# Three plain pairs instead of four in the second sequence chunk, P and Q stored in two halves, weights' jobs later

## The chip, the cores and the metric

The kernel runs on one core of one Trainium2 chip. The metric is the device time of one execution in microseconds (us), median of several runs. A profiled execution gives the trace; its span runs from the first to the last instruction. TensorE is written PE here, VectorE DVE, ScalarE ACT, GpSimd POOL and SyncE SP, as in the profile.

## The reference, cut to what matters

```python
xn = layernorm(x)                                    # x: 2048 x 512
a = einsum("bsd,ed->bse", xn, dft_hid_re)
b = einsum("bsd,ed->bse", xn, dft_hid_im)
s = einsum("ts,bse->bte", dft_seq_re, a) - einsum("ts,bse->bte", dft_seq_im, b)
h = relu(einsum("bsd,df->bsf", xn, w1) + b1) ** 2    # F = 1792
g = silu(einsum("bsf,fd->bsd", h, w2) + b2)
out = x + s * g
```

All is float32. `s` takes the sequence transform as a 2048 x 2048 product and the hidden transform as a 512 x 512 product, each with a real and an imaginary matrix.

## The kernel before

**Number format.** Every operand is split in a high part (a copy on ACT, `split_hi`, L136) and a low part (source minus high, on DVE, `split_lo`, L139), both in a format that PE multiplies fast. A product of two operands is three passes: high x high, high x low, low x high.

**Seven products.** Nearly all matrix products go as a 2 x 2 block product by seven multiplications (`PRODUCTS`) instead of eight. That needs sums of the blocks of both operands beforehand, made on DVE, and sums of the seven results afterwards, in the "closing" steps (`closing_of`).

**Stages.** (1) Layer norm of `x`, with chunk 0 of the sequence transform multiplied plainly meanwhile. (2) Chunks 1 to 7 of the sequence transform: `c` counts chunks of 256 output rows of both sequence matrices, `j` eight pairs of 128-row tiles of `x`. The sequence matrices are multiplied with `x` first; the results P and Q go to DRAM (`PQD`). (3) The Y units multiply P and Q with the hidden matrices (`WDP`). (4) The H units: first dense layer. (5) The second dense layer, SiLU, the product and the residual. The change lies in stage 2; its last effects reach the first Y units.

**Chunk 0 and the x sums.** After chunk 0 the sums of the `x` blocks must be made, for the pairs 0 to 3 in one go (`side[0]`, four steps of a generator) and for 4 to 7 in another (`side[1]`), and each pair's sums must be split (`split_sums(j)`, 1024 elements a partition, ACT and DVE), before a pair can take part in seven products.

**Chunk 1 ("second sequence chunk").** To give DVE time for that, the pairs in `MIXED` (4, 5, 6, 7) are multiplied plainly in chunk 1: `plain_step(j)`, eight block products, 48 matmuls of 256 columns, which need no sums, only a split of 1024 elements. The other pairs (0, 1, 2, 3) go by seven products, 42 matmuls, and each needs three sums of the matrix blocks (`step_sums`, L300, L302, L303) and a split of 1792 elements (`step_split`). The loop over `MIXED` (L605 to L634) lists by hand which preparations are issued at each plain pair.

**Chunks 2 to 7.** The loop over `steps` (L638 to L675): a step issues the matmuls of its pair, then the sums for two steps on (`step_sums(n + 2)`), the split for the next step (`step_split(n + 1)`), the load for four steps on (`step_load(n + 4)`, into a tile `u` of three buffers), then a closing step of the chunk before, then jobs of the table `EARLY`. The split operands use two buffers, `ga` and `gb`, in turn by the parity of `j`, so the split of a step can begin only when PE has finished the step before the present one. All engines take their instructions in this order; one that waits holds what is queued behind it on its engine. DMA loads and stores of this stage are all issued on SP.

**Closing and store.** At the last pair of a chunk (`LAST`) the result tile `e` is taken anew. ACT copies one bank to it and, but for the last chunk, three banks to `left` buffers; DVE does two closing steps, and the rest follow in the next chunk, one a step by `LATER` and `LATER_1` (the latter for the closing of chunk 1, which has one step more). At `j == 5` of that next chunk, one DMA of 1 MB stores `e` (L660). `e` is one buffer, so the next chunk's closing waits for that store to land. The layout of `e` has C12 and C11 in its first half, C22 and C21 in its second.

**Jobs of `EARLY`.** `d0` to `d3`: the hidden matrices, `v0`, `v1`, `v6`: parts of `w1`. Each (`weight`, L435) has five steps: load, first sum, other two sums, split and store of three blocks (768 elements a partition), split and store of four blocks of sums (1024). The split operands lie in `wd0` or `wd1`. `p0` to `p3` load transformed hidden matrices back (`load_wd`, L495; `p0` into `wd0`, `p1` into `wd1`) in two halves. `y0` to `y2` (`y_early`, L480) prepare the first P and Q tiles for the Y units: load, sums, split of three blocks, split of four.

**Into the Y units.** After the step (7,7) come two closing steps and the last three steps of `y2`; then the Y units (`YUnit`), whose first group of 12 matmuls is followed on ACT by a "seed" copy and on DVE by sums.

Of the kernel before, what the change touches and what calls it, by code (L numbers as in the profile page):

```python
# [16 lines left out]
NJ, NP = NS // 2, NF // 2  # L17
CW = 256
NC = S // CW
TC = 512  # L20
NTC = S // TC
WARM = 8, 5
MIXED = 4, 5, 6, 7

REST = NP - 4

# [8 lines left out]


EARLY = {
# [8 lines left out]
}  # L46
LATER = {0: 1, 1: 1, 2: 1, 3: 1, 4: 1}
LATER_1 = {0: 1, 1: 1, 2: 1, 3: 1, 4: 1, 5: 1}


Y_SIDE = (
# [73 lines left out]
C21, C11, C22, C12 = range(4)  # L125
# [5 lines left out]
def fnet_gated_kernel(ctx, tc, x, xt, ct, wd, w1, w2, b1, b2, out):  # L131
    nc = tc.nc
    ctx.enter_context(tc.manual_schedule(engines=None))

    def split_hi(hi, lo, src):
        nc.scalar.activation(hi, src, AF.Copy)  # L136
# [4 lines left out]
    def split(*parts):  # L141
        split_hi(*parts)
        split_lo(*parts)
# [15 lines left out]
    PQD = [dram.tile([P, 2, 4, 256], F32, name=f"pqd{c}") for c in range(NC)]  # L159
# [30 lines left out]
    XC = [None] * NJ  # L190
# [85 lines left out]
    def split_sums(j):  # L276
        s = xn32[j].rearrange("p h (b n) -> p (h b) n", b=2)
        split(XC[j][:, S2:S1 + 1, HI, :], XC[j][:, S2:S1 + 1, LO, :], s)
# [9 lines left out]
    def plain_parts(c, j, hs=slice(0, 2)):  # L288
        if (c, j) not in part:
            part[c, j] = operand_buf("g" + "ab"[j % 2], f"g{c}_{j}", 0 if c or j == NJ - 1 else 3 if j in TURNED else 1, (2, 4, CW))  # L290
        g, r = part[c, j], raw[c, j]
        s = slice(2 * hs.start, 2 * hs.stop)
        return g[:, HI, s], g[:, LO, s], r[:, s]
# [11 lines left out]
    def sums_a(*operands):  # L305
        list(sums_a_steps(*operands))

    def sums_a_steps(t, a21, a11_a22, a11, a12, turned=False):

        nc.vector.tensor_tensor(t[:, 0:2], a21.to_broadcast([P, 2, 256]), a11_a22, op=ALU.subtract)  # L310
        yield
        if turned:
            nc.vector.tensor_tensor(t[:, 2], a11, t[:, 1], op=ALU.subtract)
            nc.vector.tensor_tensor(t[:, 3], a12, t[:, 2], op=ALU.subtract)  # L314
        else:
            nc.vector.tensor_tensor(t[:, 2], t[:, 1], a11, op=ALU.subtract)
            nc.vector.tensor_tensor(t[:, 3], t[:, 2], a12, op=ALU.add)  # L317

    def sums_rows(t, r, turned=False):

        sums_a(t, r[:, C12:C12 + 1], r[:, C11:C22 + 1], r[:, C11], r[:, C21], turned)

    def sums_w1_steps(t, r):
        return sums_a_steps(t, r[:, 0:1], r[:, 1:4:2], r[:, 1], r[:, 2], True)
# [10 lines left out]
    def step_sums(n):  # L335
        if n < len(steps):
            u = raw[steps[n]]
            sums_b(u[:, 4:8], u)
# [44 lines left out]
    def mm(ps, w, mv, first, last):  # L383

        ps = ps.rearrange("p (i d t) -> p d i t", i=2, d=2)
        for d in range(2):
            for a_, b_ in PASSES:
                nc.tensor.matmul(ps[:, d], w[:, a_, d * P:(d + 1) * P], halves(mv(b_)),  # L388
                                 start=first and d == 0 and (a_, b_) == (HI, HI),
                                 stop=last and (a_, b_) == (LO, HI), skip_group_check=True)  # L390
# [17 lines left out]
    ms = {}  # L408
# [9 lines left out]
                mm(ms[k], XC[j][:, a], lambda b_: g[:, b_, q], j == MIXED[0] and not i, k == Z and j == MIXED[-1] and i == 1)  # L418

    one, two = slice(0, 1), slice(1, 2)  # L420
    steps = [(1, j) for j in range(NJ) if j not in MIXED] + [(c, j) for c in range(2, NC) for j in range(NJ)]
    order = [(0, j) for j in range(NJ)] + [(1, j) for j in MIXED] + steps
    making, makers = {}, {}

    def go(*names):


        for v in names:
            if v[0] == "h" and int(v[1:]) >= NTC * NP:
                continue  # L430
            if v not in making:
                making[v] = makers[v[0]](int(v[1:]))
            next(making[v])
# [46 lines left out]
    def y_early(n):  # L480

        k = n // 2
        r = buf(f"pq{k}0", [P, 4, 256], f"yr{n}")
        load_pq(n, r)
        yield
        t = buf(f"pq{k}1", [P, 4, 256], f"yt{n}")
        sums_rows(t, r, True)
        yield
        g = yop[n] = operand_buf(Y_HOME[n // 2 % 3][n % 2], f"yg{n}", 1 if n % 6 else 3)
        split(g[:, HI, 4:7], g[:, LO, 4:7], r[:, 0:3])  # L490
        yield
        split(g[:, HI, 0:4], g[:, LO, 0:4], t)
        yield
# [51 lines left out]
    g = plain_parts(0, 1)  # L545
# [3 lines left out]
    side = sums(0), sums(1)  # L549
    load_c(0, 3)  # L550
    load_x(4)
    for j in range(1, NJ):
# [31 lines left out]
        g = plain_parts(*order[j + 1])  # L584
# [16 lines left out]
    def some(steps_, n):  # L601
        for _ in range(n):
            next(steps_)

    for i, j in enumerate(MIXED):  # L605
        if i == 0:
            some(side[0], 2)
            split(*plain_parts(1, MIXED[1]))
            split_sums(0)
            for k in range(ND):  # L610
                plain_out(k)
            for k in range(2):
                nc.sync.dma_start(PQD[0][:, k].rearrange("p k n -> p (k n)"), plain[k])
            some(side[1], 1)
        elif i == 1:
            split_sums(1)
            split(*plain_parts(1, MIXED[2]))
            some(side[1], 1)
            split_sums(2)
            go("d0")  # L620
        elif i == 2:
            split_sums(3)
            some(side[1], 1)
            split(*plain_parts(1, MIXED[3]))
            step_sums(0)
            go("d0", "d0")
        else:
            step_sums(1)
            some(side[1], 1)
            step_split(0)  # L630
            split_sums(4)
            split_sums(5)
        plain_step(j)
        load_c(*order[NJ + i + 4])  # L634

    LAST = {(c, max(j for c_, j in steps if c_ == c)) for c in range(1, NC)}
    closing = None
    for n, s in enumerate(steps):  # L638
        c, j = s
        if c > 1 and j == 0:  # L640
            ms = {}
        for k, tag in banks(c).items():
            if k not in ms:
                ms[k] = bank(tag, f"m{k}_{c}")
        g = part.pop(s)
        for p in FIRST if j == 0 and c > 1 else ORDER:
            a, b = PRODUCTS[p]
            mm(ms[p], XC[j][:, a], lambda b_: g[:, b_, b], j == 0 and (c > 1 or p in (1, 5, 6, 7)), s in LAST)
        step_sums(n + 2)
        step_split(n + 1)  # L650
        if n < 2:
            split_sums(6 + n)
        if n == 0:
            e = buf("e", [P, 2048], "c1")
            copy(chunk_part(e)(C22), halves(ms[Z]))
        step_load(n + 4)
        if closing:
            some(closing, (LATER_1 if c == 2 else LATER).get(j, 0))
            if j == max(LATER_1):
                nc.sync.dma_start(PQD[c - 1].rearrange("p h k n -> p (h k n)"), e)  # L660
                closing = None
        if s in LAST:
            if c > 1:
                e = buf("e", [P, 2048], f"c{c}")
            room = {}
            if c < NC - 1:
                room = buf("pq10", [P, 2, 512], f"left{c}")
                room = {7: room[:, 0], 5: room[:, 1], 3: buf("pq11", [P, 512], f"left3_{c}")}
            closing = closing_of(chunk_part(e), ms, room, c == 1)
            some(closing, 2)  # L670
        if s == (2, 4):
            nc.vector.transpose(stats_t, stats.rearrange("p m h j -> p (m h j)"))
            for q in range(4):
                nc.sync.dma_start(rows[:, q * 32:(q + 1) * 32], stats_t[q * 32:(q + 1) * 32, :])
        go(*EARLY.get(s, ()))  # L675
# [326 lines left out]
    for u in range(2, NC):  # L1002
        n = 2 * u + 2
# [41 lines left out]
    for n in range(NTC * NP):  # L1045
        unit = HUnit(n)
        first, second, later = H_SIDE.get(n, ((), (), ()))
# [15 lines left out]
        if n == NTC * NP - 1:  # L1063
            ms = Banks(0)
# [22 lines left out]
    for n in range(NTC * NP):  # L1087
        c, p = divmod(n, NP)
        last = c == NTC - 1
        if n and not last and p == 0:  # L1090

            ms = Banks(c)
            for k in (2, 4, 5):
                bias(ms[k], k)
        elif last and p == 0:

            ms = {k: bank(t, f"m{k}_last") for k, t in
                  {1: "b20", 2: "b21", 6: "b30", 7: "b31", 5: "bb", 3: "ba"}.items()}
# [27 lines left out]
        if p == NP - 1 and not last:  # L1126
            e = buf("e", [P, 4, 512], f"z{c}")
# [16 lines left out]
    e = buf("u", [P, 4, 512], f"z{c}")  # L1144
# [95 lines left out]
```

## Time and profile before

| | us |
|---|---|
| median of 3 runs | 676.29 (676.10 to 677.19) |
| profiled execution, its time | 673.96 |
| profiled execution, its span | 672.1 |
| PE busy | 663.7 |
| DVE busy | 608.0 |
| ACT busy | 381.0 |

A line of the timeline gives the start of a run of like instructions, its length, engine, source line, operation, the tiles as out<-in, the shapes and the count; in square brackets, the idle time of the engine ahead of it and what ended that idle time. Lengths of instructions that follow each other without a gap overlap a little, since an engine starts the next before the last has drained; so a price is best read from start to start. A line of a helper such as L139 or L388 stands for all uses of the helper; the tile names tell them apart. In the table of DMA issues the last number is the median time from issue to landing.

### The profile page before, as it was taken

To read this page: it belongs to the slowest core of one execution; us is meant where nothing else is said; L and a number is where in the kernel's file an instruction comes from. 1 tells how busy PE (TensorE), PEld (TensorE's weight loads), DVE (VectorE), ACT (ScalarE), POOL (GpSimd) and SP (SyncE) were. 2 spreads that over 40 slices of the span, in tenths; PEclk is the share of its full clock that TensorE was granted. 3 is DMA by queue.
4 is the path that set the end of the run, shared out by engine and by line. 5 is a ranking of instruction groups with operands and counts; after the bars stand their busy time and mean duration, and the time that the engine had idled before them with its cause. 6 is when DMAs were issued, how large, how long until landed. Compare 5 with 4: busy or idle time off the path is not lost.

```text
span 672.1 us, 13519 instructions
## 1 busy us (share of the span) xinstructions
PE 663.7 (99%) x5605; PEld 651.5 (97%) x5605; DVE 608.0 (90%) x844; ACT 381.0 (57%) x516; POOL 8.8 (1%) x11
## 2 busy tenths in 40 slices
PE   8999999999999999999999999999999999999997
PEld 5889999999999999999899999999999999999997
DVE  7998999899989999998799988977887889999997
ACT  6855563535445454544365547788778765454451
POOL 0000000000000000000000000000000000101010
PEclk9999999999999999999999999999999999999999
DMA  8735264948659485879488668576755866677775
GB/s 284 234 105 186 87 219 145 325 138 285 238 184 352 150 282 193 280 271 319 157 298 279 201 188 299 199 262 214 267 182 196 328 241 211 179 232 194 215 204 157
DMA packets 51741, 150.85 MB, mean 224 GB/s; under 512 B 4960, under 2 KB 19552, under 8 KB 50272
## 3 DMA queue, kind: packets, MB, share of 16 engines
q1 hardware_dynamic: 43568, 129.28, 57.6%
q10 hardware_dynamic: 6208, 18.88, 7.1%
q0 software_dynamic: 1904, 1.84, 1.9%
q8 instruction: 44, 0.72, 0.4%
q14 instruction: 17, 0.14, 0.1%
HBM read 101.98 MB, written 47.99 MB: 223 GB/s over the span
## 4 chain that ended last, share of the span: by engine, by line
PE 89%; DVE 6%; DMA 2%; ACT 2%; issue 1%; SPq 0%; DVEq 0%; ACTq 0%
PE m L388 34%; PE m_o L905 15%; PE r_B L799 13%; PE r_A L799 9%; PE pq_b L399 4%; PE r_C L799 4%; PE r_D L799 4%; PE m_last L905 4%; PE pq_bb L399 1%; DMA pqd<-c 1%; DVE g L139 1%; DMA x<-in_x 1%; DVE c L373 1%; DVE xc L139 1%; DVE xn L273 1%
## 5 line engine op out<-in xcount | busy, mean ns | idle before, releaser
L388 PEld LDWEIGHTS m<-g,xc 128*128 128x128 f32 x2376 | 270.1, 188 | 0.9 <-DVE g L139 0.5
L388 PE MATMUL m<-g,xc 128*128 128x256 f32 x2376 | 270.6, 276 | 0.3 <-DVE g L139 0.3
L136 ACT ACTIVATE g<-u 128x1792 fp32r<-128x1792 f32 (+2 forms) x65 | 101.6, 1564 | 132.4 <-PE m L388 85.3
L139 DVE TENSOR_TENSOR g<-u,g 128x1792 fp32r<-128x1792 f32 (+2 forms) x66 | 120.0, 1819 | 9.1 <-ACT g L136 8.9
L905 PE MATMUL m_o<-w,g 128*128 128x256 f32 x882 | 100.5, 276 | 0.0
L905 PEld LDWEIGHTS m_o<-w,g 128*128 128x128 f32 x882 | 100.3, 188 | 0.0
L136 ACT ACTIVATE g<-hr 128x1792 fp32r<-128x1792 f32 (+2 forms) x31 | 48.2, 1565 | 40.0 <-DVE hr L317 17.8
L799 PE MATMUL r_B<-xT,w 128*128 128x256 f32 x504 | 66.5, 276 | 0.0
L799 PEld LDWEIGHTS r_B<-xT,w 128*128 128x128 f32 x504 | 61.5, 188 | 0.0
L139 DVE TENSOR_TENSOR g<-hr,g 128x1792 fp32r<-128x1792 f32 (+2 forms) x31 | 56.7, 1838 | 2.9 <-ACT g L136 2.8
L799 PE MATMUL r_A<-xT,w 128*128 128x256 f32 x336 | 43.1, 276 | 0.0
L399 PE MATMUL pq_b<-g,xc 128*128 128x512 f32 x144 | 41.2, 392 | 1.4 <-DVE small L247 1.4
L799 PEld LDWEIGHTS r_A<-xT,w 128*128 128x128 f32 x336 | 40.3, 188 | 0.2 <-DVE xT L139 0.2
L799 PE MATMUL r_B<-wdp,yg 128*128 128x256 f32 x288 | 36.0, 277 | 1.4 <-ACT r_B L146 1.2
L300 DVE TENSOR_TENSOR u<-u 128x512 f32<-128x512 f32 x52 | 35.6, 685 | 0.8 <-DMA u<-in_ct 0.7
L799 PEld LDWEIGHTS r_B<-wdp,yg 128*128 128x128 f32 x288 | 34.1, 188 | 1.8 <-ACT r_B L146 1.4
L399 PEld LDWEIGHTS pq_b<-g,xc 128*128 128x128 f32 x144 | 26.7, 188 | 8.1 <-ACT g L136 2.2
L905 PE MATMUL m_last<-w,g 128*128 128x256 f32 x294 | 33.5, 276 | 0.0
L905 PEld LDWEIGHTS m_last<-w,g 128*128 128x128 f32 x294 | 33.4, 188 | 0.0
L139 DVE TENSOR_TENSOR yg<-yraw,yg 128x1792 fp32r<-128x1792 f32 x13 | 26.2, 2018 | 0.8 <-ACT yg L136 0.8
L136 ACT ACTIVATE yg<-yraw 128x1792 fp32r<-128x1792 f32 x13 | 22.2, 1710 | 7.9 <-DVE yraw L314 7.3
L302 DVE TENSOR_TENSOR u<-u 128x256 f32<-128x256 f32 x52 | 22.1, 425 | 1.8
(185 smaller groups left out, 835.0 us busy)
## 6 DMA issues: line engine op xcount, KB each, us to landing
u<-in_ct SPq DMA_DIRECT2D x63, 512.0 KB, 3.8
hd<-h ACTq DMA_DIRECT2D x28, 512.0 KB, 5.1
hr<-hd SPq DMA_DIRECT2D x28, 512.0 KB, 3.7
pqd<-c SPq DMA_DIRECT2D x7, 1024.0 KB, 7.6
wdp<-wdd SPq DMA_DIRECT2D x8, 896.0 KB, 7.2
yraw<-pqd SPq DMA_DIRECT2D x13, 512.0 KB, 5.7
w<-w1d SPq DMA_DIRECT2D x6, 896.0 KB, 8.1
y<-y ACTq DMA_DIRECT2D x8, 512.0 KB, 4.9
```

The source lines that it names most:

```text
L136: nc.scalar.activation(hi, src, AF.Copy)
L139: nc.vector.tensor_tensor(lo, src, hi.bitcast(F32), op=ALU.subtract)
L273: nc.vector.tensor_tensor(s[:, :, to], s[:, :, a], s[:, :, b], op=op)
L300: nc.vector.tensor_tensor(t[:, 0:2], r[:, 0:1].to_broadcast([P, 2, 256]), r[:, 1:3], op=ALU.add)
L302: nc.vector.tensor_tensor(t[:, 2], t[:, 1], r[:, 1], op=ALU.add)
L373: nc.vector.tensor_tensor(part_(to), halves(room.get(m, ms[m])), part_(frm), op=op)
L388: nc.tensor.matmul(ps[:, d], w[:, a_, d * P:(d + 1) * P], halves(mv(b_)), start=first and d == 0 and (a_, b_) == (HI, HI), stop=last and ( ...
L399: nc.tensor.matmul(accs[k], w, part[0, j][:, b_, 2 * h:2 * h + 2], start=j == 0 and h == 0 and (a_, b_) == (HI, HI), stop=j == NJ - 1 and ...
L799: nc.tensor.matmul(self.region(REGION[k]), w, mv, start=i == 0 and k in (1, 7), stop=i == len(ops) - 1, skip_group_check=True)
L905: nc.tensor.matmul(m[:, i * 256:(i + 1) * 256], ready[n][:, a_, H_SLOT[a], i * P:(i + 1) * P], W2[p][:, b_, b], start=p == 0 and i == 0 an ...
```

## The change

- In chunk 1 the pairs 4, 5 and 6 stay plain, and five pairs go by seven products, in the order 1, 0, 3, 2, 7 (`SEVEN`), which keeps the parities in turn.
- The splits of the `x` sums move: those of pairs 0 and 1 are issued at the first plain pair, 2 at the second, 3 at the third, and the rest during steps 1 to 5 of the loop over `steps`, by `SUMS_AT`: 7, 4, 5, and 6 (in the first step of chunk 2).
- The weights' jobs begin later: only the load of `d0` is issued in chunk 1, and the rest of `d0` starts at (2,2). The whole table `EARLY` follows, up to (7,0).
- The sums of `y_early` become two steps.
- The closing of chunk 1 takes two steps at `j == 1`, so that every closing is through at `j == 4`, and its first half at `j == 3`. `e` is stored in two halves of 512 KB, at `j == 3` and `j == 4`.

```diff
-MIXED = 4, 5, 6, 7
+MIXED = 4, 5, 6
+SEVEN = 1, 0, 3, 2, 7
+SUMS_AT = {1: 7, 2: 4, 3: 5, 5: 6}
...
 EARLY = {
-    (1, 2): ("d0", "d1"), (2, 0): ("d0",), (2, 1): ("d1",), (2, 3): ("d1",), (2, 4): ("d1", "d2"), (2, 6): ("d1",),
-    (3, 0): ("d2",), (3, 1): ("d2",), (3, 2): ("d2", "d3"), (3, 4): ("d2",), (3, 5): ("d3",), (3, 6): ("d3", "d3", "v0"),
-    (4, 1): ("d3",), (4, 2): ("v0",), (4, 3): ("p1",), (4, 4): ("v0",), (4, 6): ("v0", "v1"), (4, 7): ("p1",),
-    (5, 0): ("v0",), (5, 1): ("v1",), (5, 3): ("v1",), (5, 4): ("v1", "v6"), (5, 6): ("v1",),
-    (6, 0): ("v6",), (6, 1): ("v6",), (6, 2): ("v6", "y1"), (6, 4): ("v6",), (6, 6): ("y1", "p0"),
-    (7, 0): ("p0",),
-    (7, 1): ("y1", "p3"), (7, 2): ("p3",), (7, 3): ("y1", "y0", "p2"), (7, 4): ("y2", "p2"), (7, 5): ("y0", "y0"),
-    (7, 6): ("y0",), (7, 7): ("y2", "y2", "y2"),
+    (2, 2): ("d0",), (2, 3): ("d0",), (2, 5): ("d0", "d1"), (2, 6): ("d0",), (3, 0): ("d1",), (3, 1): ("d1",),
+    (3, 2): ("d1", "d2"), (3, 4): ("d1",), (3, 5): ("d2",), (3, 6): ("d2", "d2", "d3"), (4, 1): ("d2",), (4, 2): ("d3",),
+    (4, 4): ("d3",), (4, 5): ("d3", "v0"), (4, 6): ("d3",), (4, 7): ("p1",), (5, 0): ("v0",), (5, 1): ("v0", "p1"),
+    (5, 2): ("v0", "v1"), (5, 4): ("v0",), (5, 5): ("v1",), (5, 6): ("v1", "v1", "v6"), (6, 1): ("v1",), (6, 2): ("v6",),
+    (6, 4): ("v6",), (6, 5): ("v6", "y1"), (6, 6): ("v6",), (6, 7): ("p0",), (7, 0): ("y1", "p0"),
+    (7, 1): ("y1", "p3"), (7, 2): ("y1", "p3"), (7, 3): ("y0", "p2",), (7, 4): ("y1", "y2", "p2"), (7, 5): ("y0", "y0"),
+    (7, 6): ("y0", "y0"), (7, 7): ("y2", "y2", "y2", "y2"),
 }
 LATER = {0: 1, 1: 1, 2: 1, 3: 1, 4: 1}
-LATER_1 = {0: 1, 1: 1, 2: 1, 3: 1, 4: 1, 5: 1}
+LATER_1 = {0: 1, 1: 2, 2: 1, 3: 1, 4: 1}
...
-steps = [(1, j) for j in range(NJ) if j not in MIXED] + [(c, j) for c in range(2, NC) for j in range(NJ)]
+steps = [(1, j) for j in SEVEN] + [(c, j) for c in range(2, NC) for j in range(NJ)]
...
         t = buf(f"pq{k}1", [P, 4, 256], f"yt{n}")
-        sums_rows(t, r, True)
+        first = sums_rows_steps(t, r, True)
+        next(first)
+        yield
+        list(first)
         yield
...
     for i, j in enumerate(MIXED):
         if i == 0:
             some(side[0], 2)
+            some(side[1], 1)
             split(*plain_parts(1, MIXED[1]))
             split_sums(0)
+            split_sums(1)
             for k in range(ND):
                 plain_out(k)
             for k in range(2):
                 nc.sync.dma_start(PQD[0][:, k].rearrange("p k n -> p (k n)"), plain[k])
+        elif i == 1:
+            step_sums(0)
+            split(*plain_parts(1, MIXED[2]))
+            split_sums(2)
             some(side[1], 1)
-        elif i == 1:
-            split_sums(1)
-            split(*plain_parts(1, MIXED[2]))
-            some(side[1], 1)
-            split_sums(2)
-            go("d0")
-        elif i == 2:
-            split_sums(3)
-            some(side[1], 1)
-            split(*plain_parts(1, MIXED[3]))
-            step_sums(0)
-            go("d0", "d0")
         else:
             step_sums(1)
             some(side[1], 1)
             step_split(0)
-            split_sums(4)
-            split_sums(5)
+            split_sums(3)
+            go("d0")
...
         step_sums(n + 2)
         step_split(n + 1)
-        if n < 2:
-            split_sums(6 + n)
+        if n == 0:
+            some(side[1], 1)
+        elif n in SUMS_AT:
+            split_sums(SUMS_AT[n])
...
         if closing:
             some(closing, (LATER_1 if c == 2 else LATER).get(j, 0))
-            if j == max(LATER_1):
-                nc.sync.dma_start(PQD[c - 1].rearrange("p h k n -> p (h k n)"), e)
+            if j in (3, 4):
+                q = slice((j - 3) * 1024, (j - 2) * 1024)
+                nc.sync.dma_start(PQD[c - 1][:, j - 3].rearrange("p k n -> p (k n)"), e[:, q])
+            if j == 4:
                 closing = None
```

More of the change, by code (lines that the diff above doesn't have):

```diff
@@ L317, in sums_a_steps, with sums_rows_steps, sums_rows @@
             nc.vector.tensor_tensor(t[:, 3], t[:, 2], a12, op=ALU.add)
-    def sums_rows(t, r, turned=False):
-        sums_a(t, r[:, C12:C12 + 1], r[:, C11:C22 + 1], r[:, C11], r[:, C21], turned)
+    def sums_rows_steps(t, r, turned=False):
+        return sums_a_steps(t, r[:, C12:C12 + 1], r[:, C11:C22 + 1], r[:, C11], r[:, C21], turned)
+    def sums_rows(*operands):
+        list(sums_rows_steps(*operands))
     def sums_w1_steps(t, r):
@@ L630, in fnet_gated_kernel @@
             step_split(0)
-            split_sums(4)
-            split_sums(5)
+            split_sums(3)
+            go("d0")
         plain_step(j)
         load_c(*order[NJ + i + 4])
-    LAST = {(c, max(j for c_, j in steps if c_ == c)) for c in range(1, NC)}
+    LAST = {(1, SEVEN[-1])} | {(c, NJ - 1) for c in range(2, NC)}
     closing = None
@@ L647, in fnet_gated_kernel @@
             a, b = PRODUCTS[p]
-            mm(ms[p], XC[j][:, a], lambda b_: g[:, b_, b], j == 0 and (c > 1 or p in (1, 5, 6, 7)), s in LAST)
+            mm(ms[p], XC[j][:, a], lambda b_: g[:, b_, b], (c > 1 and j == 0) or (not n and p in (1, 5, 6, 7)), s in LAST)
         step_sums(n + 2)
         step_split(n + 1)
-        if n < 2:
-            split_sums(6 + n)
+        if n == 0:
+            some(side[1], 1)
+        elif n in SUMS_AT:
+            split_sums(SUMS_AT[n])
         if n == 0:
```

## The prediction, made before the changed kernel ran

> **What bounds the kernel.** I read the engines' busy time first, then the chain that ended last. A step is written (chunk, x pair).
>
> ```profile
> PE 663.7 (99%) x5605; PEld 651.5 (97%) x5605; DVE 608.0 (90%) x844; ACT 381.0 (57%) x516; POOL 8.8 (1%) x11
> PE 89%; DVE 6%; DMA 2%; ACT 2%; issue 1%; SPq 0%; DVEq 0%; ACTq 0%
> ```
>
> TensorE (PE) is the bound, and the vector engine (DVE) runs close behind. So time can come only from fewer matmuls or from places where PE waited. The pace of PE without waits is in the chain's pieces (start, length):
>
> ```profile
> 536.82 97.94 PE m_o L905 x864
> ```
>
> 97.94 / 864 = 0.11336 us for a matmul of 256 columns: 5.44 for a plain pair (48), 4.76 for a pair by seven products (42), 1.36 for a group of 12. I held every stretch against that. The stretches that are too long:
>
> First, PE in the second chunk (timeline: start, length), and the scalar engine's (ACT) high-part pass, which is released when PE has finished a step and so marks the steps' ends:
>
> ```profile
> 51.62 26.81 PE L388 MATMUL m<-g,xc 128*128 128x256 f32 x235
> 78.74 5.44 PE L388 MATMUL m<-g,xc 128*128 128x256 f32 x44 [0.31 <-DVE g L139]
> ```
> ```profile
> 73.64 1.71 ACT L136 ACTIVATE g<-u 128x1792 fp32r<-128x1792 f32 x1 [0.57 <-ACT xc L136]
> 78.40 1.70 ACT L136 ACTIVATE g<-u 128x1792 fp32r<-128x1792 f32 x1 [1.62 <-PE m L388]
> 83.92 1.71 ACT L136 ACTIVATE g<-u 128x1792 fp32r<-128x1792 f32 x1 [2.87 <-PE m L388]
> ```
>
> From 73.64 to 78.40 is 4.76, as it should be; from 78.40 to 83.92 is 5.52, **0.76 lost**. PE waited for DVE's low-part pass of (1,1):
>
> ```profile
> 75.15 0.68 DVE L300 TENSOR_TENSOR u<-u 128x512 f32<-128x512 f32 x1
> ...
> 76.67 2.02 DVE L139 TENSOR_TENSOR g<-u,g 128x1792 fp32r<-128x1792 f32 x1
> 78.60 1.22 DVE L139 TENSOR_TENSOR xc<-xn,xc 128x1024 fp32r<-128x1024 f32 x1
> 79.73 0.69 DVE L300 TENSOR_TENSOR u<-u 128x512 f32<-128x512 f32 x1
> ```
>
> DVE is back to back here, and start to start gives its prices: the sums of a step 1.52, a low pass of 1792 elements 1.93, one of 1024 elements 1.13.
>
> Second, where chunk 2 ends (ACT):
>
> ```profile
> 126.76 1.71 ACT L136 ACTIVATE g<-u 128x1792 fp32r<-128x1792 f32 x1 [2.11 <-issue]
> 130.74 0.60 ACT L146 ACTIVATE c<-m 128x512 f32<-128x512 f32 x1 [2.28 <-DMA pqd<-c]
> ...
> 136.57 1.70 ACT L136 ACTIVATE g<-u 128x1792 fp32r<-128x1792 f32 x1 [1.66 <-PE m L388]
> 141.69 1.71 ACT L136 ACTIVATE g<-u 128x1792 fp32r<-128x1792 f32 x1 [3.42 <-PE m L388]
> ```
>
> Three steps took 14.93 for 14.28, **0.65 lost**: ACT's first copy of the closing sums waited until the store of the chunk before had left the buffer `e`; the bank behind that copy is the one (3,0) multiplies into first.
>
> Third, the same store at the end of chunk 7, at the start of the Y units (PE, then SP, ACT, DVE):
>
> ```profile
> 322.41 1.67 PE L799 MATMUL r_A<-wdp,yg 128*128 128x256 f32 x12
> 323.91 1.52 PE L799 MATMUL r_D<-wdp,yg 128*128 128x256 f32 x12
> 326.61 1.63 PE L799 MATMUL r_B<-wdp,yg 128*128 128x256 f32 x12 [1.18 <-ACT r_B L146]
> ...
> 332.57 1.65 PE L799 MATMUL r_B<-wdp,yg 128*128 128x256 f32 x12 [0.25 <-DVE y L809]
> 334.06 1.52 PE L799 MATMUL r_A<-wdp,yg 128*128 128x256 f32 x12
> ```
> ```profile
> 312.47 0.44 SPq L660 DMA_DIRECT2D pqd<-c  x1
> ```
> ```profile
> 321.75 0.60 ACT L146 ACTIVATE c<-m 128x512 f32<-128x512 f32 x1 [6.03 <-DMA pqd<-c]
> ...
> 325.23 1.06 ACT L136 ACTIVATE yg<-yt 128x1024 fp32r<-128x1024 f32 x1 [2.14 <-DVE yt L314]
> 326.19 0.37 ACT L146 ACTIVATE r_B<-r_A 128x256 f32<-128x256 f32 x1
> ```
> ```profile
> 322.39 1.29 DVE L373 TENSOR_TENSOR c<-m,c 128x512 f32<-128x512 f32 x2 [4.41 <-ACT c L146]
> ...
> 328.98 3.20 DVE L373 TENSOR_TENSOR c<-m,c 128x512 f32<-128x512 f32 x5
> 332.10 0.41 DVE L809 TENSOR_TENSOR y<-r_B,y 128x256 f32<-128x256 f32 x1
> ```
>
> Seven groups of 12 from 322.41 to 334.06 took 11.65 for 9.52, **2.13 lost**. Store at 312.47, ACT held 6.03 until 321.75, DVE idle 4.41 behind it, the preparation of y2 late by that much, the seed copy r_B behind it late, and the sum at 332.10 behind five closing sums late.
>
> **The change, part by part.**
>
> *Matmuls.* One plain pair of 48 becomes one pair of 42: 6 x 0.11336 = **0.68 less** on PE.
>
> *Work beside it.* The pair costs DVE one more group of sums and a low pass of 1792 for one of 1024: 1.52 + 0.80 = 2.32, and ACT some 0.7 by the same ratio. It is free only if DVE stays ahead of PE, which now comes to the seven-product steps one plain step earlier. I ran DVE's new order through by these prices, from its first pass of the chunk:
>
> ```profile
> 52.91 1.23 DVE L139 TENSOR_TENSOR g<-u,g 128x1024 fp32r<-128x1024 f32 x1 [1.98 <-ACT g L136]
> ```
>
> One x sum now fits into the 1.98 idle ahead of it. Then to the low pass of (1,1): two plain passes, three of the x sums' low passes, two x sums (seven of 1.13), two groups of step sums (3.04) and the pass (1.93), 12.9, which with two waits of some 0.3 on ACT ends near 66.4. PE wants it at 51.62 + 3 x 5.44 = 67.94. After that a step of DVE is 1.52 + 1.93 + one pass or x sum of 1.13 = 4.58 in 4.76, and the low pass cannot end before ACT's high pass: 0.25 after the step's start, plus 1.71, plus 1.93, so 3.9 into a step, 0.86 before PE wants it. The 0.76 goes, because two of the six low passes of x sums (1.13 each) that stood ahead of the second such step now stand behind it, and the weight sums (1.5) have left the chunk. Late next would be the same pass, by whatever exceeds 0.86.
>
> The load of (1,0) stands behind the stores of P and Q of chunk 0, which come one ACT pass (1.0) later than before, so it goes at about 57.2 for 56.22 (SP); then the landing times of such loads and stores:
>
> ```profile
> 56.22 0.41 SPq L286 DMA_DIRECT2D u<-in_ct  x1
> ```
> ```profile
> u<-in_ct SPq DMA_DIRECT2D x63, 512.0 KB, 3.8
> pqd<-c SPq DMA_DIRECT2D x7, 1024.0 KB, 7.6
> ```
>
> It lands near 61.0; DVE wants it at 61.8. No cost, and 1.5 more of margin at (1,1).
>
> *Chunks 2 to 7.* Weight jobs keep their instructions and transfers, two to eight steps later each; the Y job's sums are cut in two with the same three instructions. In chunk 2 the x sums' pass of pair 6 takes the place of a weight pass of equal size. Chunk 5 gets the job pattern that chunk 3 had and keeps; its densest step (two weight parts, 1.8, on 3.45) has light ones on both sides. Chunk 3 before, by ACT's high passes four steps apart:
>
> ```profile
> 146.47 1.71 ACT L136 ACTIVATE g<-u 128x1792 fp32r<-128x1792 f32 x1 [2.34 <-PE m L388]
> 165.46 1.71 ACT L136 ACTIVATE g<-u 128x1792 fp32r<-128x1792 f32 x1 [2.27 <-PE m L388]
> ```
>
> 18.99 for 19.04: nothing lost, so nothing is to be expected of chunk 5. Cost 0; the cover is PE's step, and if it went, the excess over 0.86 in a step would show.
>
> *The stores.* Six more issues on SP, of about 0.4 each, while SP waits for DVE anyway; behind each half in SP's queue are the step's weight jobs and the next load, which waits four us longer for a low pass. The first half is issued two steps earlier, the last one step (4.76) earlier, so the last of chunk 6 at about 307.7. Landing times of all transfers to and from this tensor (min/median/max):
>
> ```profile
> DMA to landing us min/median/max: 2.6/6.2/9.2
> ```
>
> Even at 9.2 it has left `e` by 316.9; ACT wants `e` at about 318.7, when the first product of (7,7) is done. So ACT's 6.03 goes, and DVE is some 3.5 earlier: in us from the units' start it has its two first closing sums done at -1.8, y2's sums at -0.3, y2's passes (one waits 1.0 for ACT) at 1.9, y3's sums at 3.4, the five closing sums at 6.6. The seed copy follows its product at once; the sum that PE waited for follows product 5 (6.8) at 7.4, where PE wants its bank at 8.16. **2.13 goes**, and with the same wait at chunk 2's end the **0.65**. Next late would be the low pass of y3 (1.93 more), at 9.3 where unit 1 starts at 9.5.
>
> *The sum.* 0.68 + 0.76 + 0.65 + 2.13 = 4.22. The profiled execution spans 672.1 and took 673.96, so it would take 669.7; the median of the runs is 676.29, 2.3 above it, and I take the difference over: **672.1**.
>
> The Trainium skill (Trainium Kernel Development and Optimization, Performance Expectations) calls matmul busy time a bad metric, because matmuls are pipelined. Read by the idle marks of the matmul rows alone, the stalls are 0.31 + 1.18 + 0.25 = 1.74 and the sum 2.42; by the starts it is 4.22, and this trace agrees with the rule: the wait marked 0.31 cost a step 0.76.
>
> **Rivals.**
>
> *Half of it.* Only what the matmul rows mark as idle returns: 0.68 + 1.74 = 2.42, 673.9. For it: restart costs may appear elsewhere, and y3 has 0.2 of margin. Against: spacing of starts is time.
>
> *The store is not what holds ACT.* The wait is put down to the semaphore that came last; were it another, only 0.68 + 0.76 = 1.44 stays, 674.85. Against: ACT's wait ends 9.2 after the issue, the landing time of that store.
>
> *DVE late in chunk 1.* It has 0.18 per step to spare. If each low pass waits, the 0.76 stays and the added 2.32 comes onto PE: 4.22 - 0.76 - 2.32 = 1.14, 675.15.
>
> *Slower: SP held by a weight store.* The load of the transformed weights into `wd1` and `wd0` is now issued one step after the last store out of the same buffer, at (4,7) and (6,7), where before it was two. SP would stand until that store has landed, and the loads of `u` behind it. Stores and loads of these tensors (min/median/max), and one such store's issue:
>
> ```profile
> DMA to landing us min/median/max: 4.5/5.4/9.3
> ```
> ```profile
> DMA to landing us min/median/max: 5.0/7.1/10.2
> ```
> ```profile
> 271.00 0.52 SPq L451 DMA_DIRECT2D w1d<-w16g  x1
> ```
>
> 271.00 is 5.7 into (6,4), which starts 12 steps before 322.41. A store of S frees SP at 5.7 + S; the next load lands 4.2 later; DVE wants it four steps on, at 19.04, with 0.86 to spare. So PE loses S - 10.0 at each of the two places: 0.2 at the slowest row, nothing at the medians. It decides from S = 12.1, where both take back 4.22; slower by 0.2% from 12.8; at 14, 8.0 - 4.22 = 3.8 over, 680.1.
>
> The granted clock is at its top in all 40 slices:
>
> ```profile
> PEclk9999999999999999999999999999999999999999
> ```
>
> The Trainium skill (TensorE: Matmul & The Clock Gate, What's actually happening) halves PE's clock after an idle window of some 3.4 us; by that, an estimate from the page, each such place would cost up to 1.7 more. No run here shows it.
>
> **How the numbers follow.** Forecast 0.62 (its own range 671.2 to 673.0), half of it 0.20, store not the holder 0.07, DVE late 0.06, slower 0.05. About 0.2%, 1.35 us, is what a measurement can tell from no change, so faster means under 674.94. Faster: 0.62 + 0.20 + two thirds of 0.07 = 0.86; same 0.09; slower 0.05. The range takes in the first two cases: from 671.2 (0.2 for the lowest run shown, 0.7 because median and profiled run stand 2.3 apart) to 673.9 + 0.9, the spread above the median: 674.8.
>
> **What would show it.** PE without an idle mark from 51.6 to the end, and high passes 4.76 apart from (1,1) to (7,7); ACT's closing copies with no wait for the store; the Y units' groups 1.36 apart from their first. I am wrong if PE waits for DVE in chunks 1 or 5, if ACT still waits for a half store, or if loads land late after (4,7) or (6,7).

## The result and the profile after

The changed kernel took 670.15 us (median of 5 runs, 669.43 to 671.63); the kernel before, beside it, 676.26 (5 runs, 673.65 to 677.19). The ratio is 0.9924, with a 95% interval from 0.9899 to 0.995: faster, and 1.05 us below the low end of the forecast range. Over the runs of this study the medians are 675.02 for the kernel before (66 runs; four single executions of it further down, 672.96 to 675.27, are not among them) and 670.15 for the changed one (17 runs), 4.87 apart.

| | before | after |
|---|---|---|
| profiled execution, time | 673.96 | 669.43 |
| its span | 672.1 | 667.7 |
| PE busy | 663.7 | 662.3 |
| DVE busy | 608.0 | 610.7 |

The page of the changed kernel, engines and the chain that ended last:

```profile
PE 662.3 (99%) x5599; PEld 650.9 (97%) x5599; DVE 610.7 (91%) x847; ACT 382.1 (57%) x516; POOL 8.8 (1%) x11
PE 94%; DVE 5%; issue 1%; ACT 0%; DMA 0%; DVEq 0%
```

The six matmuls are gone as counted, DVE's work has grown by 2.7 us (2.32 was counted), and the transfers have left the chain. ACT's high passes in chunk 1, at the steps that stood 5.52 apart before:

```profile
67.49 1.71 ACT L137 ACTIVATE g<-u 128x1792 fp32r<-128x1792 f32 x1 [2.79 <-issue]
72.25 1.71 ACT L137 ACTIVATE g<-u 128x1792 fp32r<-128x1792 f32 x1 [2.57 <-issue]
77.01 1.71 ACT L137 ACTIVATE g<-u 128x1792 fp32r<-128x1792 f32 x1 [2.10 <-PE m L391]
```

4.76 each. ACT at the end of chunk 2, where it had waited 2.28 for the store:

```profile
124.61 1.71 ACT L137 ACTIVATE g<-u 128x1792 fp32r<-128x1792 f32 x1 [2.11 <-issue]
126.22 0.58 ACT L147 ACTIVATE c<-m 128x512 f32<-128x512 f32 x1
...
134.13 1.71 ACT L137 ACTIVATE g<-u 128x1792 fp32r<-128x1792 f32 x1 [2.54 <-PE m L391]
138.89 1.71 ACT L137 ACTIVATE g<-u 128x1792 fp32r<-128x1792 f32 x1 [3.05 <-DVE wd1t L303]
```

The copy follows at once, and three steps take 14.28. The start of the Y units: PE, then ACT, then DVE, then SP's last half store of chunk 6:

```profile
319.82 1.52 PE L803 MATMUL r_A<-wdp,yg 128*128 128x256 f32 x12
321.18 1.52 PE L803 MATMUL r_D<-wdp,yg 128*128 128x256 f32 x12
322.54 1.52 PE L803 MATMUL r_B<-wdp,yg 128*128 128x256 f32 x12
...
327.98 1.52 PE L803 MATMUL r_B<-wdp,yg 128*128 128x256 f32 x12
329.34 1.52 PE L803 MATMUL r_A<-wdp,yg 128*128 128x256 f32 x12
```
```profile
315.94 0.60 ACT L147 ACTIVATE c<-m 128x512 f32<-128x512 f32 x1 [2.01 <-PE m L391]
...
321.38 0.37 ACT L147 ACTIVATE r_B<-r_A 128x256 f32<-128x256 f32 x1 [0.77 <-PE r_A L803]
```
```profile
316.68 1.32 DVE L376 TENSOR_TENSOR c<-m,c 128x512 f32<-128x512 f32 x2 [0.36 <-ACT c L147]
...
323.31 3.20 DVE L376 TENSOR_TENSOR c<-m,c 128x512 f32<-128x512 f32 x5
326.89 0.42 DVE L813 TENSOR_TENSOR y<-r_B,y 128x256 f32<-128x256 f32 x1 [0.38 <-PE r_B L803]
```
```profile
305.41 0.42 SPq L663 DMA_DIRECT2D pqd<-c  x1
```

ACT's closing copy waits for PE and no longer for the store; the seed copy waits for PE; so does the DVE sum that PE had waited for. Seven groups take 9.52, as without waits.

**A measure for the rest.** From the first matmul of chunk 1 to the start of the eighth group of the Y units, less the matmuls between at 0.11336, is what PE lost there. For the kernel before: 334.06 - 51.62 - (2376 x 0.11336 + 9.52) = 3.58. For the changed one: 329.34 - 50.91 - (2370 x 0.11336 + 9.52) = 0.25. This "loss" is given for each trace below.

### The profile page after: what moved, and what is told of

Read it like the earlier page. It is cut to its first block, busy times and chain, and to the rows that moved or that the text cites. A ratio compares the mean times of both kernels' runs of the same rounds, so it can differ in the third digit from the quotient of the medians.

```text
span 667.7 us, 13533 instructions
## 1 busy us (share of the span) xinstructions
PE 662.3 (99%) x5599; PEld 650.9 (97%) x5599; DVE 610.7 (91%) x847; ACT 382.1 (57%) x516; POOL 8.8 (1%) x11
## 4 chain that ended last, share of the span: by engine, by line
PE 94%; DVE 5%; issue 1%; ACT 0%; DMA 0%; DVEq 0%
PE m L391 40%; PE m_o L909 14%; PE r_B L803 13%; PE r_A L803 9%; PE pq_b L402 5%; PE r_C L803 4%; PE r_D L803 4%; PE pq_bb L402 2%; DVE g L140 1%; PE warm L529 1%; DVE z L959 1%; DVE z L359 1%; DVE z L1159 0%; DVE hr L311 0%; DVE z L964 0%
```

## The experiments

Medians in us. Each kernel is compared with runs of the kernel before that were taken together with it.

### Control: the kernel before

No edit.

> The kernel before, unchanged, as a control and for a second trace. Theory A (the excess of the plain runs over the first profiled run, 2.3 us, is a longer wait for the store of P and Q at the start of the Y units, since landing times vary): ratio 1.000, and wherever this execution's span exceeds 672.1, the stretch of seven groups at the start of the Y units is longer than 11.65 by most of the excess. Theory B (the excess comes from elsewhere, as the first loads of x): that stretch stays near 11.6, and the excess stands ahead of chunk 1.

Measured: 674.81 (12 runs) beside 675.01 (21 runs), ratio 0.9993 (0.998 to 1.0006). Span 672.2, loss 4.06. It adds to the question of what varies: this execution lost 0.48 more than the first one and still had the same span, since its chunk 0 was shorter. The 0.48 is the store's: PE stood 0.47 ahead of the first group of the Y units, behind ACT's copy, which waited 6.60 for the store (6.03 in the first trace). So it lies where theory A looks for it, although the stretch of seven groups itself, 11.66, is no longer than before. Three more traces of the same kernel:

> The kernel before, one more trace. Theory A (its plain runs scatter by 0.9 us, the changed kernel's by 0.6, because the landing of the stores of P and Q is on its path): where the span differs from 672.1, the difference lies in the stretch from the last third of chunk 7 to the eighth group of the Y units and at the ends of chunks 1 to 6, with ACT's wait for the store longer there. Theory B: it lies ahead of chunk 1 (first loads) or after the Y units.

> As for the look before this one: theory A puts the difference between spans at the stores of P and Q, theory B ahead of chunk 1 or behind the Y units.

> As for the first look: theory A puts the difference between spans at the stores of P and Q, theory B ahead of chunk 1 or behind the Y units.

Measured: times 675.18, 675.27, 674.91; spans 673.4, 673.4, 673.1; losses **5.40, 5.45, 4.67**. The time ahead of chunk 1 differs by 0.7 at most (50.94 to 51.62). So the difference lies in chunks 1 to 7 and at the start of the Y units, as theory A has it, but not only in the stores. In the second and third of them ACT waited 7.00 and 6.69 for the last store, and PE stood 0.86 and 0.56 ahead of the first group of the Y units. In the first a load of `u` came late in chunk 7 (DVE, then PE):

```profile
305.47 0.69 DVE L300 TENSOR_TENSOR u<-u 128x512 f32<-128x512 f32 x1 [1.41 <-DMA u<-in_ct]
```
```profile
309.07 14.99 PE L388 MATMUL m<-g,xc 128*128 128x256 f32 x125 [0.96 <-DVE g L139]
```

In the second the wait for the store at the end of chunk 2 was 2.46 for 2.28, and two more steps were long (ACT's high passes):

```profile
136.48 1.71 ACT L136 ACTIVATE g<-u 128x1792 fp32r<-128x1792 f32 x1 [1.66 <-issue]
141.60 1.71 ACT L136 ACTIVATE g<-u 128x1792 fp32r<-128x1792 f32 x1 [3.41 <-PE m L388]
146.55 1.71 ACT L136 ACTIVATE g<-u 128x1792 fp32r<-128x1792 f32 x1 [2.51 <-DVE c L373]
151.49 1.71 ACT L136 ACTIVATE g<-u 128x1792 fp32r<-128x1792 f32 x1 [3.24 <-PE m L388]
```

5.12, 4.95 and 4.94 for 4.76. It is tempting to put the 4.95 down to DVE, but DVE is not what sets it. From low pass to low pass DVE took 4.86 and 4.92 there (139.00, 143.86, 148.78), and in a like step of chunk 1, from 88.21 to 93.16, DVE itself stood 0.35 for ACT. PE's matmuls came further apart, and evenly so: one of these steps, and a stretch after them:

```profile
141.47 5.11 PE L388 MATMUL m<-g,xc 128*128 128x256 f32 x42
156.80 4.47 PE L388 MATMUL m<-g,xc 128*128 128x256 f32 x38
```

Less 0.28 for the last matmul of each row, that is 0.118 from start to start against 0.113, while the granted clock is 1.00 in every window of 2 us. This pace sets in behind a wait of PE and lasts to the end of that step or for some steps more. Why, and what ends it, these traces do not show. In the five traces ACT's wait ahead of that copy was 2.20 and 2.28 without the two long steps, and 2.32, 2.38 and 2.46 with them. So some 0.1 more of wait goes with 0.4 more of loss.

### The stores alone

The kernel before with `LATER_1` and the store in halves of the changed one:

```diff
-LATER_1 = {0: 1, 1: 1, 2: 1, 3: 1, 4: 1, 5: 1}
+LATER_1 = {0: 1, 1: 2, 2: 1, 3: 1, 4: 1}
...
-            if j == max(LATER_1):
-                nc.sync.dma_start(PQD[c - 1].rearrange("p h k n -> p (h k n)"), e)
+            if j in (3, 4):
+                q = slice((j - 3) * 1024, (j - 2) * 1024)
+                nc.sync.dma_start(PQD[c - 1][:, j - 3].rearrange("p k n -> p (k n)"), e[:, q])
+            if j == 4:
                 closing = None
```

> The kernel before with the stores in two halves alone (four plain pairs and the old weights' table stay). Theory A: the store terms go, 0.65 + 2.13, and the runs' excess with them: 2.8 to 4.4 us faster by medians, about 672 to 673.5, with less spread; the 0.76 at the second seven-product step stays. Theory B: 2.8 faster at most, spread as before. If the store were not what holds ACT: same as before.

Measured: 672.49 (10 runs, 671.31 to 673.39), ratio 0.9961 (0.9947 to 0.9975), 2.5 faster; loss 2.10. PE at the start of the Y units:

```profile
322.67 1.52 PE L801 MATMUL r_A<-wdp,yg 128*128 128x256 f32 x12
...
332.19 1.52 PE L801 MATMUL r_A<-wdp,yg 128*128 128x256 f32 x12
```

9.52: the 2.13 there is the store's, as forecast. The 0.76 in chunk 1 stays (ACT's high passes at 78.01 and 83.53). At the end of chunk 2 ACT's copy no longer waits for the store, and yet three steps took 14.86, 0.58 over; DVE stood 0.98 for a load of `u` there (ACT, then DVE):

```profile
127.17 1.71 ACT L136 ACTIVATE g<-u 128x1792 fp32r<-128x1792 f32 x1 [2.10 <-issue]
128.78 0.59 ACT L146 ACTIVATE c<-m 128x512 f32<-128x512 f32 x1
...
142.03 1.71 ACT L136 ACTIVATE g<-u 128x1792 fp32r<-128x1792 f32 x1 [3.24 <-PE m L388]
```
```profile
128.29 0.69 DVE L300 TENSOR_TENSOR u<-u 128x512 f32<-128x512 f32 x1 [0.98 <-DMA u<-in_ct]
```

So in this trace moving the store did not give the 0.65 back, and the gain, 2.5, is below the 2.8 to 4.4 that was expected. The kernel with the old jobs further down has the early stores too; it lost 0.11 in the same three steps (128.41 to 142.80). Further steps of 4.95 and 5.18 follow in chunks 1 and 2.

### The store whole, at its old place and one step earlier

The changed kernel with one store of 1 MB at `j == 5`, and at `j == 4`:

```diff
-            if j in (3, 4):
-                q = slice((j - 3) * 1024, (j - 2) * 1024)
-                nc.sync.dma_start(PQD[c - 1][:, j - 3].rearrange("p k n -> p (k n)"), e[:, q])
-            if j == 4:
+            if j == 5:
+                nc.sync.dma_start(PQD[c - 1].rearrange("p h k n -> p (h k n)"), e)
                 closing = None
```

> The changed kernel with the store of P and Q whole, at j = 5, as before. Both theories: only the 6 matmuls (0.68) and the stall in chunk 1 (0.76) are gained, 1.44 over the kernel before by the profiled runs, so about 674.8; under theory A its runs spread as widely as those of the kernel before.

> The changed kernel with the store whole, at j = 4: one step earlier, not halved. Whole at 307.7, the store of chunk 6 lands by 317 at the slowest row (9.2), ahead of ACT at about 316 to 318: as fast as the changed kernel within 0.5 us (670.1) if it is the earlier issue that counts; near a_whole5 if it is the halves.

Measured: at `j == 4` 671.03 (6 runs), ratio 0.9937 (0.9918 to 0.9957), loss 0.88: the earlier place is what counts. Halves add 0.8 at most (670.24 for the changed kernel in another set of runs), somewhat more than the 0.5 that was expected. At `j == 5` **679.58** (6 runs), ratio 1.0062 (1.0038 to 1.0087): 4.6 **slower** than the kernel before, loss 11.17. Both theories failed here. The longest step is (5,1), where PE stood; the profile has PE, then DVE, then SP in chunk 4, then SP's longest waits for transfers:

```profile
214.43 7.82 PE L391 MATMUL m<-g,xc 128*128 128x256 f32 x51 [2.07 <-DVE g L140]
```
```profile
210.83 0.69 DVE L301 TENSOR_TENSOR u<-u 128x512 f32<-128x512 f32 x1 [3.05 <-DMA u<-in_ct]
```
```profile
197.56 0.43 SPq L662 DMA_DIRECT2D pqd<-c  x1
198.05 0.52 SPq L454 DMA_DIRECT2D wdd<-wd3g  x1
198.61 2.11 SPq L441 DMA_DIRECT2D w10r<-in_w  x1
201.85 0.33 SPq L287 DMA_DIRECT2D u<-in_ct  x1
202.98 0.52 SPq L454 DMA_DIRECT2D wdd<-wd3g  x1
```
```profile
SPq L505 <- DMA w1d<-w16g: 6.8, 1, 6.8
SPq L505 <- DMA wdd<-wd3g: 6.4, 1, 6.4
```

In the new table the weight parts of `d3` fall on (4,5) and (4,6). With the store of P and Q at `j == 5` 1 MB, 768 KB and 512 KB were put into SP's queue in the 4.3 us ahead of the load of `u` at 201.85, which then took 8.96 to land (median of such loads in this trace 3.9). The 512 KB are themselves a load, of a part of `w1`; the other two are stores. From 200 to 210 the DMA engines were full: a busy share of 0.99 to 1.04, at 359 to 412 GB/s. And SP stood 6.4 and 6.8 behind the weight stores at (4,7) and (6,7), the very places of my slower rival. The load at 201.85 was issued ahead of that stand, which speaks for the transfers. To tell the two apart:

### The loads behind the weight stores one step later

The kernel with the store at `j == 5`, and:

```diff
-    ... (4, 7): ("p1",), (5, 0): ("v0",), ... (6, 7): ("p0",), (7, 0): ("y1", "p0"),
+    ... (5, 0): ("v0", "p1"), ... (7, 0): ("y1", "p0", "p0"),
```

> The changed kernel with the whole store at j = 5 (679.6 in the run before this) and with the two loads p1 and p0 that held SP moved one step later, to (5, 0) and (7, 0). If it was SP standing behind the weight store that made the loads of u late: both long steps (8.55 and 6.72 instead of 4.76) go, 674.5 or less. If it is the transfers themselves, stores of 2.8 MB ahead of a load of u in one queue: the load issued ahead of SP's stand is as late as it was (9 us to landing), at least one long step of 2 us or more stays at (4, 7) to (5, 0), 676 to 679.

Measured: 678.9 (9 runs), ratio 1.005 (1.0035 to 1.0066), loss 9.14. PE at the same step:

```profile
215.40 6.87 PE L391 MATMUL m<-g,xc 128*128 128x256 f32 x56 [2.33 <-DVE g L140]
```

SP's stand is gone from that place, and the long step stays. So it is the transfers themselves, stores above all, ahead of a load of `u` in one queue. Whether that load would have come sooner through another queue was not tried. SP's stand was worth 0.7 by medians, within the scatter.

In the changed kernel SP does stand at both places, as forecast:

```profile
SPq L505 <- DMA w1d<-w16g: 2.6, 1, 2.6
SPq L505 <- DMA wdd<-wd3g: 2.0, 1, 2.0
```

2.6 and 2.0, and PE loses nothing there.

### The weights' jobs at their old places

The changed kernel with the old `EARLY`, the Y job's sums in one step, and in the plain pairs:

```diff
             split_sums(2)
             some(side[1], 1)
+            go("d0")
...
             split_sums(3)
-            go("d0")
+            go("d0", "d0")
```

> The changed kernel with the weights' jobs at their old places (three steps of d0 in the plain pairs, the old table) and the Y job's sums in one step. The vector engine gets 1.5 us more by (1, 1) and 0.6 to 2.1 more in single steps of chunks 1 and 2, with 0.2 to spare in each: by the forecast it falls behind, TensorE waits 1.5 to 3.5 in chunks 1 and 2, 672 to 674. If the later jobs are not needed for the gain: 670.2 to 671.

Measured: 672.98 (7 runs), ratio 0.9967 (0.9955 to 0.998), loss 3.57: 2.7 slower than the changed kernel (670.24), within what was expected. PE in chunks 1 and 2:

```profile
73.46 29.08 PE L392 MATMUL m<-g,xc 128*128 128x256 f32 x252 [0.90 <-DVE g L141]
103.69 5.05 PE L392 MATMUL m<-g,xc 128*128 128x256 f32 x42 [1.14 <-DVE g L141]
```

Part of the first wait is a late `u` (DVE waited 1.12 for one at 62.61); the second is DVE's own load. So the later jobs are what pays for the fifth pair on DVE: with the old jobs, four plain pairs were 2.5 under the kernel before (the stores alone), three only 1.9.

### Four plain pairs, the rest of the change kept

`MIXED = 4, 5, 6, 7`, the old lists of preparations in chunk 1 without the two later steps of `d0`; halves and the new table stay.

> The changed kernel with four plain pairs and the old lists of preparations in chunk 1, but without the weights' jobs there; halves and later jobs stay. By the forecast: 0.68 slower than the changed kernel for the six matmuls, and most of the 0.76 gone all the same, since 1.5 us of weight sums have left the vector engine ahead of (1, 1): about 670.8 to 671. If the 0.76 needs the fifth pair's new order: 671.5 to 672.

> The changed kernel with four plain pairs, once more. If six matmuls are worth their time: 0.7 over the changed kernel of this call, as the traces had it (668.2 for 667.5 of span). If the fifth pair gives nothing: equal within 0.2, as the medians had it (670.30 for 670.24).

Measured: 670.30 (6 runs) beside 670.24 of the changed kernel, and a second time 670.76 (6 runs) beside 670.14; over both, means of 670.68 (12 runs) and of 670.28 (17 runs, with the first five). Losses -0.05 and 0.21: PE runs through chunk 1 without the 0.76. The two traces with four plain pairs, then the first and a second of the changed kernel (start and length of the stretch of chunks 1 to 7):

```profile
51.19 269.45 PE L390 MATMUL m<-g,xc 128*128 128x256 f32 x2376
```
```profile
50.94 269.71 PE L390 MATMUL m<-g,xc 128*128 128x256 f32 x2376
```
```profile
50.91 269.08 PE L391 MATMUL m<-g,xc 128*128 128x256 f32 x2370
```
```profile
51.16 268.77 PE L391 MATMUL m<-g,xc 128*128 128x256 f32 x2370
```

Where nothing is lost, 269.45 and 268.77 are 0.68 apart, the six matmuls. In the times 0.4 of it is seen, with scatters of 0.7 in both kernels: the pair by itself is hardly more than the noise. The kernel with four plain pairs is 4.6 under the kernel before both times (674.88 and 675.38), so nearly all of the gain comes without the fifth pair. And the 0.76 went by moving the weight sums out of chunk 1, not by the fifth pair's new order.

### The changed kernel twice more

> The changed kernel again, with more runs beside the kernel before on one chip. The terms as forecast (0.68 + 0.76 + 0.65 + 2.13 = 4.2): a ratio of 0.9937 to 0.994. If the first five runs (6.1 by medians) were the rule: 0.991.

> The changed kernel once more, beside the one with four and the one with two plain pairs: 4.6 under the kernel before, 670.2.

Measured: 670.24 (6 runs) beside 674.88 (15 runs), ratio 0.9926 (0.9911 to 0.994), loss -0.05; 670.14 (6 runs) beside 675.38 (13 runs), ratio 0.9925 (0.9908 to 0.9941), loss 1.13, most of it behind a late load of `u` where chunk 3 ends (DVE stood 1.19 for it). So it scatters by late loads as well, but less.

### One plain pair fewer still

`MIXED = 4, 5`, `SEVEN = 0, 1, 2, 3, 6, 7`, the load of `d0` at (1,2), its sums at (2,3) and (2,4), and the preparations that stand at the plain pairs and in the loop (not all lines that go are shown):

```diff
+SUMS_AT = {1: 2, 2: 3, 3: 6, 4: 7, 6: 4, 8: 5}
...
         if i == 0:
             some(side[0], 2)
             some(side[1], 1)
             split(*plain_parts(1, MIXED[1]))
             split_sums(0)
...
+            step_sums(0)
+            split_sums(1)
+            some(side[1], 1)
+        else:
+            step_split(0)
+            step_sums(1)
...
-        if n == 0:
+        if n in (0, 3):
             some(side[1], 1)
-        elif n in SUMS_AT:
+        if n in SUMS_AT:
```

> The changed kernel with one more pair taken from the plain ones: pairs 4 and 5 plain, 0, 1, 2, 3, 6, 7 by seven products. Six matmuls fewer (0.68) if the vector engine stays ahead, then 0.6 to 0.7 under the changed kernel in the same call. The vector engine has one pass of 1.13 more than slots in chunk 1 and 0.18 to spare in each step: a wait of 0.2 to 0.6 on TensorE at the step (1, 6) or (1, 7), or more if the sums of pairs 6 and 7 come late, is the rival; then no gain or up to 1 slower.

Measured: 672.16 (8 runs, 670.68 to 674.92), 2.0 slower than the changed kernel beside it (670.14); loss 4.32. PE, and the DVE pass that it waits for:

```profile
84.21 28.14 PE L391 MATMUL m<-g,xc 128*128 128x256 f32 x240 [0.76 <-DVE xc L140]
```
```profile
82.93 1.22 DVE L140 TENSOR_TENSOR xc<-xn,xc 128x1024 fp32r<-128x1024 f32 x1 [1.13 <-ACT xc L137]
```

The x sums of pair 6 are late, ACT's pass over them stands 3.23 for DVE, and their low pass comes behind that. Some 1.1 of the loss is PE's pace of 0.118 in chunks 5 and 6 alone: six steps of 4.95 from 227.70 to 257.38, in which DVE stands 0.56 and 0.79 for ACT. That order of preparations has no room for a sixth pair. No version tried beats the changed kernel.

## Why the prediction was right in its parts and too high in its time

- **Each term of the sum is gone, three of the four as forecast.** 0.68 for six matmuls (269.45 less 268.77); the 0.76 at (1,1); the 2.13 at the start of the Y units, shown to be the store's by the kernel with the stores alone. The low passes of chunk 1, y2 and the sum that PE had waited for came in time. The profiled execution, forecast at 669.7, took 669.43; that it comes so close is partly luck, as both profiled executions lie low among the runs of their kernels.
- **The 0.65 at the end of chunk 2** went too, but the store is not all that held it, as the prediction has it. With the stores alone ACT's wait was gone, and 0.58 was still lost, with a load of `u` late. With the later jobs beside the stores (four plain pairs) nothing is lost there, with the old jobs and three plain pairs 0.11. Whether the late load was chance, one trace of the stores alone does not tell.
- **The step that failed is the last one of the sum**, "the median of the runs is 676.29, 2.3 above it, and I take the difference over". Two sizes are in it. The three runs shown lay high: 66 runs have the median 675.02, 1.27 lower. And the stalls were sized from one execution, the one that lost least of five: 3.58 where the five traces lost 3.58, 4.06, 5.40, 5.45 and 4.67, 4.63 on average; longer waits for the last store in three of them, and two to four steps of 4.95 in each of the last three, are part of it. The changed kernel lost 0.25, -0.05 and 1.13, 0.44 on average. 4.63 - 0.44 + 0.68 = 4.87, which is the difference of the medians, for a forecast 4.22: 0.65 too little (the same figure as one of the terms, by chance). That it fits to the last digit is luck: averages of five and three traces are uncertain by some 0.4 each. By the medians, 1.27 + 0.65 = 1.92 is all of 672.07 - 670.15.
- The range went wrong the same way: it allowed 0.7 below for the offset of 2.3, though the reason for that offset, stalls that vary with the landing of transfers, would have told that most of it goes with the stalls. The spread says so too: 1.05 us (standard deviation) in the kernel before, 0.55 with the stores alone moved, 0.72 after, 1.55 with the whole store at `j == 5`. Why the first three runs lay as high as they did was not settled.
- **The 0.76** was put down to two things, the x sums' passes that now stand behind (1,1) and the weight sums that left. The kernel with four plain pairs shows that the second is enough.
- **Half of it** (the rows' idle marks, 2.42) was refuted: starts, not marks, are time. **The store is not the holder** was refuted by the stores alone. **DVE late** did not come in the changed kernel, and is what came with the old jobs and with two plain pairs; the margin per step was as thin as stated, though PE's pace behind a wait, and not DVE alone, makes up part of the loss there.
- **Slower by a weight store** had the place right and the mechanism half right. With the old store at `j == 5` the changed order is 4.6 slower than before, and its longest steps, (5,1) and (7,1), follow (4,7) and (6,7). But it is not SP's stand: without it the long steps stay. I had looked at SP's turn and not at what is queued in front of a load once it is issued. So the stores at `j == 3` and `j == 4` are not an extra to the moved jobs: without them these would cost more than the whole change gains.
- One small loss was overlooked: in chunk 7 three steps running carry parts of `y1`, and in the first trace PE lost 0.28 in step (7,3), where DVE had stood 0.62 for a load of `u`. The second trace, with the same parts, lost nothing there.

## What to carry to other kernels

Where one execution shows stalls that end on transfers, take their size from several traces: the one at hand is one draw, and removing the wait also removes what the plain runs lose beyond it. When jobs with stores of their own are moved, look up what will stand ahead of the next load in the same queue, by bytes, and not only whose turn it is to issue. And do not put every long step down to the engine that is nearly full: look whether that engine waits itself in such a step. Here it did, and the matmuls came evenly further apart.

## What the runs showed of the hardware

In the kernel with the whole store at `j == 5`, PE stood 2.07 us by its idle mark and then ran slower. Windows of 2 us (PE, PEld, DVE, ACT and POOL busy, granted clock, DMA share, GB/s):

```profile
212.00:214.00 2.00, 0.36 (x4) 0.16 (x2) 1.98 (x2) 1.39 (x1) 0.00 (x0) 1.00 0.08 33
214.00:216.00 2.00, 1.57 (x12) 1.57 (x13) 2.00 (x4) 0.31 (x1) 0.00 (x0) 0.97 0.74 185
216.00:218.00 2.00, 2.00 (x12) 2.00 (x11) 1.93 (x4) 0.00 (x0) 0.00 (x0) 0.50 0.99 409
218.00:220.00 2.00, 2.00 (x14) 2.00 (x14) 1.98 (x3) 0.00 (x0) 0.00 (x0) 0.68 0.36 137
220.00:222.00 2.00, 2.00 (x20) 2.00 (x19) 1.75 (x4) 0.84 (x1) 0.00 (x0) 1.00 0.90 291
```

The granted clock fell to a half after PE had begun again, and this cost 1.7 us on top of the wait (0.03 + 0.50 + 0.32 of windows of 2 us), so at half rate it lasted about 3.4 us. In the kernel with the loads one step later, a wait of 2.33 at the same place was followed by no such drop (granted clock 1.00 in every window of 2 us around it). The Trainium skill (TensorE: Matmul & The Clock Gate, What's actually happening) has such a drop after an idle window of some 3.4 us; here a shorter wait was enough once and was not enough another time.

The second thing is the pace behind a wait: 0.118 us from matmul to matmul instead of 0.113, at a granted clock of 1.00, for one step or several (six steps of 4.95 running in the kernel with two plain pairs). It is shown as a fact of these traces, and its cause is open.
